# Pooling q inside the score product of the first batch, adding the pooled part while the output is turned back, and retuning modelled transfer times

## The chip, the cores and the metric

The kernel runs on one core of one Trainium2 chip. The metric is the device time of one execution in microseconds. Most versions were executed four times next to the kernel before on the same chip; medians are given.

## The reference, cut to what matters

```python
# q, k, v: [8 batches, 8 heads, 576 tokens, 64]
q_d = q.reshape(B, H, 144, 4, D).mean(axis=3)      # and k_d, v_d: pooled over 4 tokens
out_up    = repeat(softmax_attention(q_d, k_d, v_d), 4, axis=tokens)
out_local = attention over the tokens within distance 3
x = (out_up + out_local) as [8*576 tokens, 512]
h = x @ w_in                                        # 512 -> 2048
out = (h - tanh(h)) @ w_out                         # 2048 -> 512
```

## The kernel before

The kernel treats two heads at a time as a head pair: four pairs make one batch, p0 to p3 being batch 0. In SBUF, q and k of a pair lie interleaved in bf16 (`qk[..., token, 0 or 1]`), two heads stacked in the 128 partitions, so each head is a 64-row operand of TensorE. The dense part consumes x in blocks of 512 tokens, so its first block needs all four pairs of batch 0.

Pooling and pooled scores. VectorE or GpSimd pools q and k together in two adds (`add1`, `add2`), and then four products make the pooled scores:

```python
def s2(step=16):
    biased(480, 576, t2)
    for hh in range(2):
        score(4, hh, 0, t2)
    for i in range(2):
        for hh in range(2):
            rows = slice(64 * hh, 64 * hh + 64)
            c = 96 + G * i                          # G = 144
            T.matmul(two(t2)[:, hh, c:c + G], qkd[s][rows, step * i:step * i + 128, 1],
                     qkd[s][rows, 0:G, 0], start=True, stop=True)
```

Turning back in batch 0: six transposes on TensorE, a copy of the pooled part (`od`), and two joins on VectorE that add each pooled column to four tokens:

```python
for q0, n, t in [...]:
    T.transpose(flat()[:, q0:q0 + n], ln[s][0:n, t, :], ident[0:n, 0:n])
... od[s] <- flat()[:, 480:480 + G]                 # ACT or DVE
... xT[j] <- flat()[...] + od[s] broadcast by 4     # DVE, twice
```

From batch 1 on, the turning of q and k (`qr` to `qT`) and of the output (`ln` to `lT`) is done by transposing DMAs.

The order of the instructions is not written by hand. The kernel first collects all operations with a modelled duration each, simulates the engines and the DMA queue with these, and emits the instructions in the order that the simulation gives. Where an operation may run on more than one engine (`P.choice`), the simulation picks the engine too:

```python
P.dma("SP", 1340, lambda: nc.sync.dma_start_transpose(out=qT[s], in_=...), 1684, 92, ...)
#            modelled use of the DMA engines in ns, and of one piece of it ^^^^  ^^
T_QK, T_V, ... = (760, 864), (850, 939), ...        # loads: batch 0, later batches
```

On the chip each engine has its instructions in that fixed order, whether or not the data are there; the traces below show ScalarE stand 3.25 us before a copy whose data are late, with other work queued behind it.

The softmax here doesn't subtract the row's maximum and nothing guards it: scores larger than these inputs give would overflow.

## Time and profile before

| | before |
|---|---|
| time, median of the first three runs (range) | 321.28 us (321.06 to 322.15) |
| span of the profiled execution | 321.8 us (this execution took 323.51 us) |
| TensorE busy | 307.7 us, 96% |
| first dense matmul | 25.37 us |
| TensorE idle from there to 69.2 us | 2.42 us |
| TensorE idle from 69.2 to 270 us | 2.92 us |

The idle times are window lengths minus TensorE's busy time in the window. Some matmul records are missing from each trace: of the dense products 39 are missing before, counted against their weight loads, and such a hole can show as about 0.16 us of idle time with no cause. So the sums themselves are too high.

### The profile page before, as it was taken

The page shows a single profiled execution, that of the slowest core. Times are in us where ns is not written, and L with a number is a line of the kernel's source. Part 1 is how long each engine was busy: PE and PEld are TensorE (multiplying, and loading weights), DVE is VectorE, ACT ScalarE, POOL GpSimd, SP SyncE. Part 2 cuts the span into 40 slices and gives each one's busy share as a digit, 9 for nine tenths or more (in the row PEclk, how much of TensorE's full clock was granted, in tenths as well). Part 3 has the DMA queues.
Part 4 walks back from the last instruction along what each step waited for, and adds up shares of the span by engine and source line. Part 5 has one row for each costly group of instructions (what it writes and reads, how often), then busy time and mean ns, then how long its engine had stood idle before and what let it go on. Part 6 is the DMA issues. An engine that isn't in the chain of part 4 may idle for free.

```text
span 321.8 us, 6551 instructions
## 1 busy us (share of the span) xinstructions
PE 307.7 (96%) x2370; PEld 156.6 (49%) x2411; DVE 189.4 (59%) x345; ACT 202.1 (63%) x344; POOL 178.0 (55%) x223
## 2 busy tenths in 40 slices
PE   6889989999999999999999999999999999999995
PEld 2565534655455444544544444444444544444444
DVE  5777872658855873696458634964288428443300
ACT  3876955578876885687677456775488336444411
POOL 7384335562696878688876698859679110000000
PEclk9999999999999999999999999999999999999999
DMA  7999999994979999999999999999992220000021
GB/s 229 265 249 206 223 244 266 277 253 140 209 180 208 246 233 263 253 230 227 238 236 238 226 238 232 263 203 251 217 231 56 69 80 0 33 35 33 33 98 67
DMA packets 110814, 60.13 MB, mean 187 GB/s; under 512 B 87998, under 2 KB 98110, under 8 KB 110782
## 3 DMA queue, kind: packets, MB, share of 16 engines
q1 hardware_dynamic: 106270, 54.93, 72.4%
q0 software_dynamic: 4224, 4.19, 7.7%
q10 hardware_dynamic: 288, 0.59, 0.6%
q8 instruction: 19, 0.31, 0.4%
q14 instruction: 13, 0.11, 0.1%
HBM read 43.64 MB, written 9.44 MB: 165 GB/s over the span
## 4 chain that ended last, share of the span: by engine, by line
PE 62%; DMA 17%; POOL 6%; ACT 4%; issue 4%; SPq 3%; DVE 2%; POOLq 0%; ACTq 0%; DVEq 0%
PE bank L773 29%; PE bank L739 25%; DMA vst<-in_v_dram 7%; DMA qkn<-in_k_dram 6%; PE bank L651 3%; DMA qT<-qr 3%; POOL half L567 2%; PE bank L588 2%; SPq L428 1%; POOL qkd L572 1%; ACT qk L537 1%; POOL half L475 1%; DMA lT<-ln 1%; SPq L403 1%; ACT u L748 1%
## 5 line engine op out<-in xcount | busy, mean ns | idle before, releaser
L773 PE MATMUL bank<-w_out_sb,gT 128*128 128x512 bf16 (+1 forms) x572 | 133.3, 373 | 3.2 <-DVE gT L751 1.3
L739 PE MATMUL bank<-xT,w_in_sb 128*128 128x512 bf16 x557 | 132.6, 379 | 1.1 <-issue 0.3
L751 DVE TENSOR_TENSOR gT<-bank,u 128x512 bf16<-128x512 f32 x144 | 96.2, 687 | 49.4 <-ACT u L748 48.7
L748 ACT ACTIVATE u<-bank 128x512 f32<-128x512 f32 x144 | 84.5, 606 | 41.7 <-PE bank L739 37.9
L773 PEld LDWEIGHTS <-gT 128*128 128x128 bf16 x592 | 55.3, 98 | 61.2 <-issue 1.9
L739 PEld LDWEIGHTS <-w_in_sb 128*128 128x128 bf16 x576 | 54.3, 98 | 62.7 <-issue 0.2
L628 DVE TENSOR_TENSOR bank<-bank,bias 128x960 f32<-128x960 f32 (+1 forms) x56 | 41.3, 758 | 18.8 <-PE bank L588 17.8
L567 POOL TENSOR_TENSOR half<-qk 128x576 f32<-128x576 bf16 x28 | 32.1, 1145 | 32.4 <-ACT qk L537 13.4
L785 ACT COPY y<-bank 128x512 f32<-128x512 f32 (+1 forms) x37 | 21.3, 576 | 33.6 <-PE bank L773 28.4
L518 POOL CAST qr<-qkn 128x1152 bf16<-128x1152 f32 x28 | 32.0, 1145 | 12.0 <-DMA qkn<-in_k_dram 8.7
L632 ACT ACTIVATE E<-bank 128x960 bf16<-128x960 f32 x32 | 30.9, 971 | 12.2 <-DVE bank L628 12.2
L537 ACT COPY qk<-qT 128x1152 bf16<-128x1152 bf16 x22 | 26.8, 1217 | 9.9 <-DMA qT<-qr 9.5
L678 DVE TENSOR_TENSOR ln<-bank,r 128x768 bf16<-128x768 f32 x32 | 30.5, 957 | 1.0
L701 POOL TENSOR_TENSOR xT<-lT 128x480 bf16<-128x480 bf16 x22 | 22.3, 1012 | 15.2 <-DMA lT<-ln 15.2
L676 DVE RECIPROCAL r<-bank 128x12 f32<-128x12 f32 x32 | 7.2, 227 | 36.7 <-PE bank L651 32.7
L475 POOL TENSOR_TENSOR half<-v 128x512 f32<-128x512 f32 x20 | 26.0, 1299 | 1.3
L651 PEld LDWEIGHTS <-E 128*128 128x128 bf16 x576 | 21.7, 98 | 6.8 <-ACT E L644 0.2
L453 POOL CAST vw<-vst 128x640 bf16<-128x640 f32 x21 | 15.1, 724 | 14.4 <-DMA vst<-in_v_dram 14.4
L644 ACT ACTIVATE E<-bank 128x576 bf16<-128x576 f32 x32 | 21.4, 670 | 0.0
L572 POOL TENSOR_TENSOR qkd<-half 128x288 bf16<-128x288 f32 x30 | 19.9, 665 | 2.3 <-DVE half L567 0.8
L651 PE MATMUL bank<-vw,E 128*128 128x65 bf16 x320 | 21.0, 194 | 0.0
L588 PEld LDWEIGHTS <-qk 64*128 64x128 bf16 x320 | 9.2, 94 | 14.5 <-issue 9.8
(70 smaller groups left out, 187.6 us busy)
## 6 DMA issues: line engine op xcount, KB each, us to landing
vst<-in_v_dram SPq DMA_DIRECT2D x62, 160.0 KB, 4.2
qkn<-in_q_dram SPq DMA_DIRECT2D x32, 288.0 KB, 4.4
out_dram<-y SPq DMA_DIRECT2D x35, 256.0 KB, 2.6
qkn<-in_k_dram SPq DMA_DIRECT2D x30, 288.0 KB, 4.2
v<-in_v_dram SPq DMA_DIRECT2D x20, 256.0 KB, 3.5
w_in_sb<-in_moe_w_in_dram POOLq DMA_DIRECT2D x4, 512.0 KB, 13.1
w_out_sb<-in_moe_w_out_dram POOLq DMA_DIRECT2D x4, 512.0 KB, 17.7
v<-in_v_dram SPq DMA_DIRECT2D x20, 32.0 KB, 3.3
```

Source lines behind the costliest of these rows:

```text
L475: GP.tensor_tensor(out=v2, in0=v4[s][:, :, :, 0:128], in1=v4[s][:, :, :, 128:256], op=ALU.add)
L518: op("POOL", 1160, lambda: GP.tensor_copy(out=qr[s].rearrange("p a (h d) -> p h a d", h=2), in_=qkn[sn].rearrange("p h (a d) -> p h a d", ...
L537: op("ACT", 1095, lambda: A.copy(out=full.rearrange("p (g a) i -> p g a i", a=A9), in_=qT[s].rearrange("p a (g i) -> p g a i", i=2)), read ...
L567: eng.tensor_tensor(out=half, in0=four[:, :, 0:2, :], in1=four[:, :, 2:4, :], op=ALU.add)
L628: V.tensor_tensor(out=part, in0=part, in1=bias[:, lo:hi].unsqueeze(1) .to_broadcast([128, 2, hi - lo]), op=ALU.add)
L632: op("ACT", 860, lambda: A.activation(out=e1, in_=two(t1)[:, :, 0:480], func=AF.Exp, scale=SCALE), drain=[t1], writes=[("E", e, 0)], pri=pri)
L651: T.matmul(two(to)[0:m, hh, 65 * n:65 * n + 65], E[e][0:rhs.shape[0], c:c + m], rhs, start=first, stop=last)
L678: op("DVE", 880, lambda: V.tensor_tensor(out=ln[s].rearrange("p n (h d) -> p h n d", d=D), in0=blocks()[:, :, :, 0:64], in1=r[s].unsqueeze ...
L739: T.matmul(one(tok), w_in_sb[:, dc, fc * 128:(fc + 1) * 128], xT[dc][:, kb * 512:kb * 512 + 512], start=(dc == 0), stop=(dc == N_DC - 1))
L748: op("ACT", 490, lambda: A.activation(out=u[us], in_=one(tok), func=AF.Tanh), drain=[tok], writes=[("u", us)], pri=DPRI)
L751: op("DVE", 610, lambda: V.tensor_tensor(out=gT[g][:, fc, :], in0=one(tok), in1=u[us], op=ALU.subtract), drain=[tok], reads=[("u", us)], w ...
L773: T.matmul(one(tok)[:, 0:n], gT[g][:, fc, ts * 128:ts * 128 + 128], w_out_sb[:, fc, cols:cols + n], start=(fc == 0), stop=(fc == N_FF - 1))
```

## The change

The intent is to take work off VectorE and GpSimd in the stretch before the first dense matmul. For batch 0 TensorE pools q itself: four products with every fourth token of q accumulate in PSUM, so only k is pooled by adds. And the pooled part of the output is spread over four tokens by a product with a 0/1 matrix `up`, accumulated on top of the turned-back local part, so that one copy remains. Along with this come retuned modelled transfer times, a finer cut of the second dense block, and one load of v split in two.

```diff
 def s2(step=16):
-    for i in range(2):
-        for hh in range(2):
-            T.matmul(two(t2)[:, hh, c:c + G], qkd[s][rows, step * i:step * i + 128, 1],
-                     qkd[s][rows, 0:G, 0], start=True, stop=True)
+    for i in range(2):
+        for a in range(4 if only_k else 1):
+            for hh in range(2):
+                T.matmul(two(t2)[:, hh, c:c + G], qkd[s][rows, step * i:step * i + 128, 1],
+                         four[rows, :, a, 0] if only_k else qkd[s][rows, 0:G, 0],
+                         start=(a == 0), stop=(a == 3 or not only_k))
 ...   # add1, add2 only on k (take = slice(1, 2)) for p < 4; modelled cost of s2 370 + 480
+def back_up():                                     # p < 4
+    T.matmul(summed()[:, 0:512], ln[s][:, 4, :], up[:, 0:512], start=True, stop=False)
+    for t in range(4):
+        T.matmul(summed()[:, QW * t:QW * t + QW], ln[s][0:QW, t, :], ident[...], start=False, stop=False)
+    T.matmul(summed()[:, 480:512], ln[s][0:112, 5, :], up[0:112, 512:544], start=False, stop=True)
+    T.matmul(summed()[:, 512:576], ln[s][0:112, 5, :], up[0:112, 544:608], start=True, stop=True)
+P.choice([("ACT", 520, ... A.copy(out=xs, in_=summed()[:, 0:S])),
+          ("DVE", 620, ... V.tensor_copy(out=xs, in_=summed()[:, 0:S]))], ...)
 ...   # GpSimd builds up (c_up): 2 memsets, 7 selects
-T_QK, T_V, ... = (760, 864), (850, 939), ...
+T_QK, T_V, ... = (760, 832), (850, 904), ...
 ...   # turning DMAs: 1684 -> 1622, 1128 -> 1086 (pieces 92 -> 89); v4 loads: 1000 -> 936, 125 -> 119
 ...   # piece of a weight load: 240 -> 340
-cuts = (0, 2, 3, 4) if kb == 0 else (0, 2, 4)
+cuts = (0, 2, 3, 4) if kb < 2 else (0, 2, 4)
 ...   # first load of v: rows 0:124 -> rows 0:112 and 112:124
```

`four` is a view of the interleaved `qk`: one element of the moving operand every 4 tokens x 2 (q and k) x 2 bytes = 16 bytes. The old operand, pooled q in `qkd`, has one element every 4 bytes.

More of the change, by code (lines that the diff above doesn't have):

```diff
@@ L328 @@
     warm = lT[0].rearrange("p n c -> p (n c)")[:, 0:512]
+    up = lT[1].rearrange("p n c -> p (n c)")[:, 0:608]
     r = fixed("r", [128, 2, 6], FP32, 2)
@@ L361, in c_group, with c_up @@
                          base=3, pattern=[[4, 32]], channel_multiplier=-1)
+    def c_up():
+        GP.memset(up[:, 0:512], 1.0)
+        GP.affine_select(out=up[:, 0:512], in_=up[:, 0:512], compare_op=ALU.is_ge, fill=0.0,
+                         base=0, pattern=[[1, 512]], channel_multiplier=-4)
+        GP.affine_select(out=up[:, 0:512], in_=up[:, 0:512], compare_op=ALU.is_ge, fill=0.0,
+                         base=3, pattern=[[-1, 512]], channel_multiplier=4)
+        last = up[:, 512:608]
+        GP.memset(last, 0.0)
+        for base, mult in [(16, -1)] + [(-32 - a, -4) for a in range(4)]:
+            GP.affine_select(out=last, in_=last, compare_op=ALU.not_equal, fill=1.0,
+                             base=base, pattern=[[1, 96]], channel_multiplier=mult)
     def c_pick():
@@ L421, in issue @@
                 if b == 0 and h == 0:
-                    nc.sync.dma_start(out=t[4:128, i, 0, :], in_=v[b, h, 0:124, :])
+                    nc.sync.dma_start(out=t[4:116, i, 0, :], in_=v[b, h, 0:112, :])
+                    nc.sync.dma_start(out=t[116:128, i, 0, :], in_=v[b, h, 112:124, :])
                     nc.sync.dma_start(out=t[:, i, 1:5, :], in_=win(QW - 4, 128, 4))
@@ L447, in load_w @@
         keys = [(name, f, c) for c in range(4)]
-        P.dma("POOL", 780, issue, T_W + 1200 * (f == 0 and src is moe_w_in), 240, dst=keys, after=[after], pri=W_PRI)
+        P.dma("POOL", 780, issue, T_W + 1200 * (f == 0 and src is moe_w_in), 340, dst=keys, after=[after], pri=W_PRI)
     def prep_v(p):
@@ L467, in issue @@
                             ap=[[4 * D, n], [S * D, 2], [1, 4 * D]]))
-        load(480, lambda: issue(0, 128, 0), [("v4", s, 0)], 1000, 220, -30, 16)
-        load(420, lambda: issue(128, 16, 1), [("v4", s, 1)], 125, 125, -30, 2)
+        load(480, lambda: issue(0, 128, 0), [("v4", s, 0)], 936, 220, -30, 16)
+        load(420, lambda: issue(128, 16, 1), [("v4", s, 1)], 119, 119, -30, 2)
     def pool_v4(p):
@@ L534, in attention @@
             P.dma("SP", 1340, lambda: nc.sync.dma_start_transpose(
-                out=qT[s], in_=qr[s].rearrange("p a c -> p (a c)")), 1684, 92,
+                out=qT[s], in_=qr[s].rearrange("p a c -> p (a c)")), 1622, 89,
                   src=[("qr", s, 0), ("qr", s, 1)], dst=[("qT", s)], pri=-50, lead=500)
@@ L564, in attention @@
         adders = ADDERS[p >= NEARLY]
+        only_k = p < NP
+        take = slice(1, 2) if only_k else slice(0, 2)
         def add1(eng):
-            eng.tensor_tensor(out=half, in0=four[:, :, 0:2, :],
-                              in1=four[:, :, 2:4, :], op=ALU.add)
+            eng.tensor_tensor(out=half[:, :, :, take], in0=four[:, :, 0:2, take],
+                              in1=four[:, :, 2:4, take], op=ALU.add)
         def add2(eng):
             with nc.allow_low_precision("pooled q and k"):
-                eng.tensor_tensor(out=qkd[s][:, 0:G],
-                                  in0=half[:, :, 0, :],
-                                  in1=half[:, :, 1, :], op=ALU.add)
+                eng.tensor_tensor(out=qkd[s][:, 0:G, take],
+                                  in0=half[:, :, 0, take],
+                                  in1=half[:, :, 1, take], op=ALU.add)
         P.port.update((len(P.ops), len(P.ops) + 1))
-        P.choice([(name, n1, lambda eng=eng: add1(eng)) for name, n1, _, eng in adders],
+        P.choice([(name, n1 // (1 + only_k), lambda eng=eng: add1(eng))
+                  for name, n1, _, eng in adders],
                  reads=[("qk", s, 0), ("qk", s, 5)], writes=["half"], pri=pri)
-        P.choice([(name, n2, lambda eng=eng: add2(eng)) for name, _, n2, eng in adders],
+        P.choice([(name, n2 // (1 + only_k) + 40 * only_k, lambda eng=eng: add2(eng))
+                  for name, _, n2, eng in adders],
                  reads=["half"], writes=[("qkd", s)], pri=pri)
@@ L606, in s2 @@
             for i in range(2):
-                for hh in range(2):
-                    rows = slice(64 * hh, 64 * hh + 64)
-                    c = 96 + G * i
-                    T.matmul(two(t2)[:, hh, c:c + G], qkd[s][rows, step * i:step * i + 128, 1],
-                             qkd[s][rows, 0:G, 0], start=True, stop=True)
+                for a in range(4 if only_k else 1):
+                    for hh in range(2):
+                        rows = slice(64 * hh, 64 * hh + 64)
+                        c = 96 + G * i
+                        T.matmul(two(t2)[:, hh, c:c + G],
+                                 qkd[s][rows, step * i:step * i + 128, 1],
+                                 four[rows, :, a, 0] if only_k else qkd[s][rows, 0:G, 0],
+                                 start=(a == 0), stop=(a == 3 or not only_k))
         def s12():
@@ L636, in attention @@
         if p < MERGE:
-            op("PE", 370 + 110 * (p < NP), s2, slack=late, reads=qks + [("qkd", s)],
+            op("PE", 370 + 480 * (p < NP), s2, slack=late, reads=qks + [("qkd", s)],
                fill=[t2], pri=pri)
@@ L682, in attention @@
             op=ALU.mult), drain=[to], reads=[("r", s)], writes=[("ln", s)], pri=pri)
-        tb = P.psum(1, kind)
+        tb = P.psum(1, kind) if p >= NP else None
         def flat():
@@ L694, in attention @@
             P.dma("SP", 1260, lambda: nc.sync.dma_start_transpose(
-                out=lT[s], in_=ln[s].rearrange("p n c -> p (n c)")), 1128, 92,
+                out=lT[s], in_=ln[s].rearrange("p n c -> p (n c)")), 1086, 89,
                   src=[("ln", s)], dst=[("lT", s)], pri=-50, lead=500)
@@ L713, in attention, with summed @@
                      reads=[("lT", s)], writes=[("x", b, j)], pri=pri)
+            return
+        if p < NP:
+            tb = P.psum(2, kind)
+            def summed():
+                return two(tb).rearrange("p n c -> p (n c)")
+            def back_up():
+                T.matmul(summed()[:, 0:512], ln[s][:, 4, :], up[:, 0:512],
+                         start=True, stop=False)
+                for t in range(4):
+                    T.matmul(summed()[:, QW * t:QW * t + QW], ln[s][0:QW, t, :],
+                             ident[0:QW, 0:QW], start=False, stop=False)
+                T.matmul(summed()[:, 480:512], ln[s][0:112, 5, :], up[0:112, 512:544],
+                         start=False, stop=True)
+                T.matmul(summed()[:, 512:576], ln[s][0:112, 5, :], up[0:112, 544:608],
+                         start=True, stop=True)
+            op("PE", 500, back_up, slack=late, reads=[("ln", s), ("lT", 1), "ident"],
+               fill=[tb], pri=pri)
+            xs = xT[j][:, b * S:(b + 1) * S]
+            P.choice([("ACT", 520, lambda: A.copy(out=xs, in_=summed()[:, 0:S])),
+                      ("DVE", 620, lambda: V.tensor_copy(out=xs, in_=summed()[:, 0:S]))],
+                     drain=[tb], writes=[("x", b, j)], pri=pri)
             return
@@ L745, in mm1 @@
                reads=[("w_in", fc // 4, c) for c in range(4)] +
-               [("x", b, j) for b in bs for j in range(d1 if kb == 0 else NP)],
+               [("x", b, j) for b in bs for j in range(d1 if kb < 2 else NP)],
                writes=["dense"] * (kb == 0 and fc == 3 and d1 == 4), fill=[tok], pri=5000)
@@ L816 @@
     DPRI = -1
-    T_QK, T_V, T_W, W_PRI, NEARLY = (760, 864), (850, 939), 2750, 32, NP
+    T_QK, T_V, T_W, W_PRI, NEARLY = (760, 832), (850, 904), 2750, 32, NP
     CAST_V = [[("POOL", 770, GP.tensor_copy), ("ACT", 620, A.copy)],
@@ L829 @@
     op("POOL", 2700, c_bias, writes=["bias"], pri=-97)
+    op("POOL", 2500, c_up, writes=[("lT", 1)], pri=-50)
     for i in range(2):
```

## The prediction

> **What bounds the kernel now.** I read the page first, for the engine that fills the span.
>
> ```profile
> PE 307.7 (96%) x2370; PEld 156.6 (49%) x2411; DVE 189.4 (59%) x345; ACT 202.1 (63%) x344; POOL 178.0 (55%) x223
> ...
> PE   6889989999999999999999999999999999999995
> ...
> PEclk9999999999999999999999999999999999999999
> DMA  7999999994979999999999999999992220000021
> ```
>
> TensorE is 96% busy at full clock. The only slices below 9 are the first three, the sixth and the last (slices are 8.05 us): the attention of batch 0 must be done before any dense matmul can run, and the change touches exactly that stretch. The DMA engines are also full until about slice 30. Next I cut the span at the first dense matmul, at a gap near 49 us, and in pieces after that.
>
> ```profile
> core 0: us, PE busy (x) PEld busy (x) DVE busy (x) ACT busy (x) POOL busy (x), PEclk, DMA share, GB/s
> 0.00:25.37 25.37, 20.25 (x248) 12.06 (x251) 18.37 (x71) 16.29 (x29) 16.82 (x38) 1.00 1.01 246
> 25.37:49.00 23.63, 21.82 (x179) 11.04 (x180) 18.81 (x34) 18.10 (x35) 8.88 (x10) 1.00 1.20 226
> 49.00:69.20 20.20, 19.59 (x197) 11.69 (x201) 8.18 (x16) 11.41 (x20) 11.15 (x13) 1.00 0.98 281
> 69.20:120.00 50.80, 50.02 (x407) 25.46 (x413) 38.49 (x63) 40.28 (x69) 34.75 (x41) 1.00 0.94 201
> ```
>
> From 25.37 us on TensorE idles 1.81 us up to 49 us, then 0.61, 0.78, and 2.5 us in all from 120 to 318.5 us: 5.7 us together. So the end is the start of dense work plus a fixed queue of TensorE work (1152 full-size dense matmuls, which stream at about 0.216 us each in the chain of waits, are 249 us of it, the rest later attention) plus that idle time. The change can pay in two places only: an earlier first dense matmul, or less idle time after it. What decides the first one? The timeline at that point:
>
> ```profile
> 22.99 1.82 DVE L678 TENSOR_TENSOR ln<-bank,r 128x768 bf16<-128x768 f32 x2
> 24.97 0.49 PE L692 MATMUL bank<-ident,ln 120*128 120x120 bf16 x6
> 25.37 3.41 PE L739 MATMUL bank<-xT,w_in_sb 128*128 128x512 bf16 x15
> 26.65 0.81 DVE L722 TENSOR_TENSOR xT<-bank,od 128x480 bf16<-128x480 bf16 x2
> ```
>
> L692 turns the last head pair (p3) back, L739 is the dense input product. It starts when L692 has been issued; only its fourth operand, p3's (last row, done at 27.46), comes later, and meanwhile TensorE runs other operands. But L739 also needs weights, w_in in four parts, cast on the way by a GpSimd-issued DMA. First the two GpSimd rows that lead to it, then the landing time of the issue that starts at 15.67 (view of that tensor, cut to this issue).
>
> ```profile
> 15.01 0.72 POOL L453 CAST vw<-vst 128x640 bf16<-128x640 f32 x1 [2.16 <-DMA vst<-in_v_dram]
> 15.67 1.65 POOL L440 DMA_DIRECT2D w_in_sb<-in_moe_w_in_dram  x2
> ```
>
> ```profile
> DMA to landing us min/median/max: 9.7/9.7/9.7
> ```
>
> 15.67 + 9.7 = 25.37: the weights land in the very instant at which dense work starts. The other three landings, read the same way, are 12.2, 14.0 and 17.8 us after issues at about 16.6, 18.0 and 18.8, thus near 28.8, 32.0 and 36.6. So two things now end together at 25.4 us: the attention chain and the first weights. The issue waits on purpose for the load of v of pair 2 (2.16 us of waiting in its predecessor), which the change does not touch.
>
> The largest idle piece later:
>
> ```profile
> 45.06 0.73 ACT L453 CAST vw<-vst 128x640 bf16<-128x640 f32 x1 [2.13 <-DMA vst<-in_v_dram]
> ...
> 47.06 1.02 PE L773 MATMUL bank<-w_out_sb,gT 128*128 128x512 bf16 x4 [0.96 <-DVE gT L751]
> ```
>
> ScalarE stands in order before a cast whose v has not come; three tanh of block 0 queue behind it, so gT is late and the output product L773 waits (0.96, then another 0.33 us).
>
> **What the Trainium skill says.** "TensorE: Matmul & The Clock Gate", Part 3 (The mechanism): matmuls in different row groups run concurrently, starting about 4 ns apart. The trace agrees:
>
> ```profile
> 20.17 0.29 PE L610 MATMUL bank<-qkd 64*128 64x144 bf16 x4
> ```
>
> One of these takes 223 ns, so the fourth starts 0.29 - 0.22 = 0.07 us after the first: two pairs, 60 ns apart, 60 ns being 144 columns at the rate of L739 (512 in 0.216). The next instruction follows at 20.40, 0.23 us after the first. "SBUF — State Buffer", Door 1, says SBUF has 16-byte lines and an access that crosses to a new line pays; two hits per line are needed for full rate. The new q operand takes every fourth token of interleaved bf16 q and k, a step of 16 bytes: one hit per line. The old ones step by 4 bytes; no row here shows 16. The same page, Who interferes with whom: some two-input VectorE operations and GpSimd exclude each other. The trace agrees: the second pooling add took 0.94 us on VectorE from 9.08, beside a GpSimd cast, and 0.46 from 13.78, beside none.
>
> **The change part by part, pairs p0 to p3.**
> - Pooling of q leaves VectorE. Before: add 1 128x576 is 0.76, add 2 0.46 us, about 1.2 per pair. Half the elements: 0.4 + 0.25. Over four pairs some 2.3 us of VectorE/GpSimd time.
> - Scores: 4 products become 16. Twelve more are six pairs at 60 ns, +0.36 us per pair, 1.4 us in all, if the 16-byte step is free. If it halves the rate, eight pairs at 120 against two at 60 ns, +0.84, 3.4 us in all. Both lie before the first dense matmul, where TensorE idles or runs filler (17 filler products in the order before, 13 after).
> - Turning back: 6 transposes (0.33 us to issue) become 7 products of 512 + 480 + 32 + 64 columns, 1088 at 0.42 ns, 0.46 us. Then od (0.28) and two joins (0.82 + 0.25 before overlap) become one copy of 576 f32 columns. A ScalarE copy of 512 is 0.58, a VectorE operation on 512 f32 0.69; I estimate 0.7 us. Thus about 0.4 us less on the chain of each pair, and no two-step wait.
> - GpSimd builds the up-matrix after the bias: one memset and two selects on 512 columns (0.5 + 0.6 + 0.6, from the bias rows) and a memset and five selects of 96 (5 x 0.27): 3.3 us, from 5 to 8.4 us. The early casts of p0 and p1 that it did there go to ScalarE and VectorE instead, by the changed order. The clash with VectorE may cost p0 and p1 0.3 us.
> - Loads: the same bytes, one more small v issue. Later order changes because the modelled DMA times change.
>
> Now the chain with the changed instruction order. p3's k lands at about 13.5 as before. ScalarE no longer casts it (0.58), so exp of p2 starts near 13.9 instead of 14.16. TensorE has p1's 16 products at 12.4 to 12.9, p2's until 15.3; p3's transposes then run 15.3 to 15.8 (before 15.16 to 15.7). Two output products follow; scores of p3 at 17.5, its exp at 17.9 (before 18.19). Back-turn of p0, v pooling and 16 products bring TensorE to 19.8; p3's second exp ends at 20.8 (before 21.4), its output product at about 21.5 (before 22.3), both normalizations at 23.4 (before 24.8), back-turn at 24.0, a score step of pair 4 to 24.3. So all x could be ready by 24.7 and dense work could start near 24.3, 1.0 us earlier.
>
> But the weights. Their issue stays at 15.7, their landing at 25.4. I therefore give the earlier chain almost nothing: first dense matmul at 25.2 to 25.6.
>
> What remains is idle time. In the changed order all 16 tanh of block 0 stand before the cast that waits for v, and the joins of p2 and p3 (1.6 us of VectorE from 24.8) are gone when gT begins. That should remove most of the 1.3 us of waiting of L773. Blocks later should be neutral: same work, DMA full as before.
>
> Sum: 0 for the start, -1.1 for the stall, 0 for the rest: 321.28 - 1.1 = 320.2 us.
>
> **Rivals.**
> 1. The weights do not hold (w_in lands sooner, or the coincidence at 25.37 is chance): the full 1.0 us comes on top, 319.2. For it: L692 ended issuing only 0.08 us before. Against it: landing and start agree to 0.01 us.
> 2. The 16-byte step halves the products' rate: +0.48 us for each pair on a TensorE that p1 to p3 already queue on. The chain then ends at 25.5 to 26 instead of 24.3, and takes over from the weights: 320.4 to 320.9. Only the page speaks for it.
> 3. Supply: everything before 240 us is also near the DMA limit (share about 1). Dense work that runs ahead then waits for batch 1's x, or for w_in part 4 (lands 36.6; the new order wants it about 37.7, and GpSimd issues parts 2 to 4 about 1 us later). The gain is given back: 321.3, or 322 if a reordered queue is unlucky.
>
> **Range and chances.** Everything movable is about 2 us downwards (start and stall) and 1 us up, plus reordering noise of some 0.7 us in the 3.9 us of idle time after 49 us. Range 318.6 to 321.9. 2% is 6.4 us, more than all the idle time after the start: faster 0.02, same 0.96, slower 0.02.
>
> **What would show it.** The first L739 at 25.2 to 25.6 while the last copy of x is done before 25.2; w_in's first landing at that start. The 16 products: issue in 0.5 to 0.6 us if the step is free, about 1 us if not. No wait of L773 near 45 us, and TensorE idle from the first dense matmul to 49 us down from 1.81 to about 0.7. I am wrong if the first dense matmul comes before 24.8 or after 26, or if idle time after 69 us moves by over 1 us.

## More of the kernel before

The comparisons named e to h ran on four different chips, so a difference between medians of two comparisons is rough.

The windows of the kernel before from 120 us on (start and end, length, then busy time with instruction count of TensorE, its weight loads, VectorE, ScalarE and GpSimd, granted clock, DMA share, GB/s):

```profile
120.00:170.00 50.00, 49.42 (x401) 24.93 (x407) 30.09 (x47) 34.81 (x57) 41.10 (x49) 1.00 1.00 243
170.00:220.00 50.00, 48.89 (x366) 24.01 (x372) 31.71 (x51) 33.17 (x55) 38.64 (x45) 1.00 1.13 231
220.00:270.00 50.00, 49.55 (x346) 24.12 (x351) 27.41 (x43) 28.83 (x51) 26.65 (x33) 1.00 0.54 131
```

TensorE has almost no gap here. And one group of the page, ScalarE copying q and k from where the transposing DMA put them (busy time and mean ns, then idle time of the engine just before the group and what ended it):

```profile
L537 ACT COPY qk<-qT 128x1152 bf16<-128x1152 bf16 x22 | 26.8, 1217 | 9.9 <-DMA qT<-qr 9.5
```

Of the 22 copies some find their transposed data not yet landed; ScalarE stands 9.5 us in all. In this kernel that wait costs TensorE next to nothing.

## The result, and the profile after

The changed kernel takes **333.41 us** (median of 4 runs, 331.66 to 334.42) against 321.17 us (320.28 to 322.15) of the kernel before in the same comparison: ratio 1.0375, 95% interval 1.0321 to 1.0428, so slower by over 2%. Ratios are computed as the mean time of one kernel's fast runs over that of the other's of the same rounds, so not quite the ratio of the medians quoted beside them.

The page of the kernel after:

```profile
PE 316.4 (95%) x2418; PEld 159.8 (48%) x2459; DVE 188.1 (57%) x342; ACT 201.2 (60%) x339; POOL 181.5 (55%) x232
...
PE   6999999999999989999999798999999999999995
```

TensorE is still the full engine, but it does 8.7 us more, and the dips moved: the first slices are fuller, and there are new dips in the middle (slices 15, 23 and 25, of 8.3 us each). Its windows, cut at the new first dense matmul:

```profile
0.00:31.55 31.55, 28.03 (x298) 15.07 (x299) 17.97 (x71) 15.99 (x26) 18.42 (x44) 0.95 1.06 250
31.55:69.20 37.65, 37.33 (x332) 20.49 (x336) 24.13 (x42) 25.73 (x49) 18.52 (x21) 1.00 1.02 228
69.20:120.00 50.80, 49.20 (x412) 25.62 (x414) 35.62 (x59) 39.30 (x68) 34.01 (x41) 1.00 0.86 194
120.00:170.00 50.00, 48.51 (x405) 24.20 (x411) 29.89 (x48) 33.50 (x55) 40.17 (x46) 1.00 1.14 241
170.00:220.00 50.00, 46.47 (x342) 22.56 (x348) 32.08 (x52) 33.94 (x57) 38.96 (x46) 1.00 1.04 223
220.00:270.00 50.00, 47.84 (x365) 23.60 (x370) 27.35 (x44) 29.00 (x49) 31.45 (x39) 1.00 0.72 158
```

With these and the windows of before, the difference of the profiled spans (332.7 - 321.8 = 10.9 us) splits into the parts below. Idle time is what is left of a window, so the sum has to close; what the table tells is the split. The profiled execution of the changed kernel is the slowest of its four (334.42 us).

| | before | after | difference |
|---|---|---|---|
| first dense matmul | 25.37 | 31.55 | +6.18 |
| idle from there to 69.2 us | 2.42 | 0.32 | -2.10 |
| idle from 69.2 to 270 us | 2.92 | 8.78 | +5.86 |
| idle from 270 us to the end | 3.64 | 3.65 | 0.0 |
| TensorE busy after the first dense matmul | 287.44 | 288.40 | +0.96 |

So there are two losses of about the same size, a late start and late idle time, and one gain, the stall near 45 us that the prediction expected to vanish.

**The late start.** Rows of the timeline of the kernel after (start, length, engine, line, operation; in brackets the idle time before it and what ended that). Line 630 is the pooled products, 666 the exp of the pooled scores, 584 the first pooling add of p3 (128x288 is k alone), 757 the one copy of x that is left, 784 the dense input product:

```profile
10.38 2.21 PE L630 MATMUL bank<-qk,qkd 64*128 64x144 bf16 x16
12.62 0.65 ACT L666 ACTIVATE E<-bank 128x576 bf16<-128x576 f32 x1 [1.39 <-PE bank L630]
...
22.02 0.66 POOL L584 TENSOR_TENSOR half<-qk 128x288 f32<-128x288 bf16 x1 [5.54 <-ACT qk L569]
...
24.65 2.21 PE L630 MATMUL bank<-qk,qkd 64*128 64x144 bf16 x16
26.90 0.65 ACT L666 ACTIVATE E<-bank 128x576 bf16<-128x576 f32 x1 [1.70 <-PE bank L630]
...
30.50 1.59 DVE L757 CAST xT<-bank 128x576 bf16<-128x576 f32 x2
31.55 2.55 PE L784 MATMUL bank<-xT,w_in_sb 128*128 128x512 bf16 x11
```

The sixteen products of a pair take 2.21 us where I had expected 0.5 to 0.6, or 1 us at worst, and they do so in all four pairs. ScalarE waits for each of them (6.4 us in all), the whole chain of batch 0 is pushed back, and the last copy of x ends at 32.09 instead of 27.46 us. The first weights are no longer what holds: issued at 15.56 and landing 8.4 us later, they are there at 23.96. One thing besides the products differs: TensorE's granted clock in this profile was 0.50 from about 15.4 to 18.7 us, with TensorE busy all the while, and 1.00 in the profile of before. Up to about 1.7 us of the late start may be the clock (an estimate: half of these 3.3 us).

**The late idle time.** The same two views as before, first the groups of the page:

```profile
L784 PE MATMUL bank<-xT,w_in_sb 128*128 128x512 bf16 x558 | 135.3, 379 | 5.2 <-DVE gT L796 4.3
...
L552 ACT COPY qk<-qT 128x1152 bf16<-128x1152 bf16 x22 | 26.7, 1214 | 19.6 <-DMA qT<-qr 16.3
```

ScalarE now stands 16.3 us before the copies of transposed q and k, against 9.5, and TensorE stands 4.3 us before dense input products, waiting for VectorE's gT to free a PSUM bank; in the kernel before there was no such wait after 69 us. That the two belong together is seen in the longest one (timeline of the kernel after; line 793 is tanh, 796 is gT = h - tanh h):

```profile
182.65 1.17 ACT L552 COPY qk<-qT 128x1152 bf16<-128x1152 bf16 x1 [3.25 <-DMA qT<-qr]
183.73 1.57 ACT L793 ACTIVATE u<-bank 128x512 f32<-128x512 f32 x3
184.35 1.89 DVE L796 TENSOR_TENSOR gT<-bank,u 128x512 bf16<-128x512 f32 x3 [2.89 <-ACT u L793]
185.10 0.81 PE L784 MATMUL bank<-xT,w_in_sb 128*128 128x512 bf16 x3 [1.84 <-DVE gT L796]
```

Read it downwards: the transposing DMA is late, the copy that needs it stands first in ScalarE's queue, three tanh queue behind it and then run without a wait of their own, VectorE has no tanh to subtract, no bank comes free, and TensorE stands 1.84 us. The other three waits for gT (0.86, 0.30 and 1.31 us, ending at 117.32, 218.69 and 250.18 us) come the same way: each ends some 2.5 us after the start of such a copy (at 114.84, 216.24 and 247.72 us) that had waited 2.24, 1.10 and 2.27 us for its DMA. The landing time of these transposing DMAs was 4.5 us in the median before (3.5 to 5.4) and 5.1 us after (3.2 to 6.9); the modelled time for them had been lowered.

### The profile page after: what moved, and what is told of

Its sections match the earlier page's. It is cut to its first block, busy times and chain, and to the rows that moved or that the text cites. A ratio compares the mean times of both kernels' runs of the same rounds, so it can differ in the third digit from the quotient of the medians.

```text
span 332.7 us, 6660 instructions
## 1 busy us (share of the span) xinstructions
PE 316.4 (95%) x2418; PEld 159.8 (48%) x2459; DVE 188.1 (57%) x342; ACT 201.2 (60%) x339; POOL 181.5 (55%) x232
## 5 line engine op out<-in xcount | busy, mean ns | idle before, releaser
L784 PE MATMUL bank<-xT,w_in_sb 128*128 128x512 bf16 x558 | 135.3, 379 | 5.2 <-DVE gT L796 4.3
L818 PEld LDWEIGHTS <-gT 128*128 128x128 bf16 x592 | 56.0, 98 | 61.6 <-issue 0.3
L584 POOL TENSOR_TENSOR half<-qk 128x576 f32<-128x576 bf16 (+1 forms) x29 | 32.8, 1130 | 48.7 <-ACT qk L569 28.4
L552 ACT COPY qk<-qT 128x1152 bf16<-128x1152 bf16 x22 | 26.7, 1214 | 19.6 <-DMA qT<-qr 16.3
L468 POOL CAST vw<-vst 128x640 bf16<-128x640 f32 x22 | 16.3, 744 | 12.6 <-DMA vst<-in_v_dram 12.5
L589 POOL TENSOR_TENSOR qkd<-half 128x288 bf16<-128x288 f32 (+1 forms) x29 | 19.1, 660 | 1.1
```

The source lines that it names most:

```text
L552: op("ACT", 1095, lambda: A.copy(out=full.rearrange("p (g a) i -> p g a i", a=A9), in_=qT[s].rearrange("p a (g i) -> p g a i", i=2)), read ...
L584: eng.tensor_tensor(out=half[:, :, :, take], in0=four[:, :, 0:2, take], in1=four[:, :, 2:4, take], op=ALU.add)
L784: T.matmul(one(tok), w_in_sb[:, dc, fc * 128:(fc + 1) * 128], xT[dc][:, kb * 512:kb * 512 + 512], start=(dc == 0), stop=(dc == N_DC - 1))
L818: T.matmul(one(tok)[:, 0:n], gT[g][:, fc, ts * 128:ts * 128 + 128], w_out_sb[:, fc, cols:cols + n], start=(fc == 0), stop=(fc == N_FF - 1))
```

## The experiments

All kernels agree with the reference within the tolerance of the comparison, also those that compute a wrong pooled q. Theories at the start: **step** (the 16-byte step of the moving operand makes the products slow), **count** (sixteen products instead of four are the cost, whatever their step), **turning back** (the new product and copy cost), **order** (the new modelled times make a worse order). First the whole in one table, sorted by what was changed. "Products" is the length of the row of pooled products of one pair, "qT wait" is how long ScalarE stood for the transposing DMA between 69 and 270 us.

| kernel | q pooled by | modelled times | time, us | ratio to before | products, us | first dense, us | qT wait, us |
|---|---|---|---|---|---|---|---|
| before | adds | old | 321.17 to 323.61 | 1 | 0.29 (4) | 25.37 | 9.5 |
| after | TensorE, 16 B | lowered | 333.41 | 1.0375 | 2.21 (16) | 31.55 | 16.3 |
| e1_q_step4 | TensorE, 4 B (wrong) | lowered | 328.47 | 1.0219 | 0.68 (16) | 24.36 | 20.3 |
| e2_turn_only | adds | lowered | 328.31 | 1.0204 | | 24.95 | 17.6 |
| e3_q_only | TensorE, 16 B | old | 329.70 | 1.0242 | 2.21 (16) | 30.01 | 8.1 |
| e4_tuning_only | adds | lowered | 327.62 | 1.0205 | | 24.73 | 17.1 |
| f2_times_only | adds | lowered | 327.17 | 1.0174 | | 24.15 | 18.8 |
| f3_cuts_only | adds | old | 321.87 | 1.0005 | | 27.90 | 2.7 |
| f4_turn_old_times | adds | old | 321.20 | 0.9996 | | 25.62 | 6.1 |
| g1_after_old_times | TensorE, 16 B | old | 327.12 | 1.0169 | 2.21 (16) | 31.33 | 6.2 |
| g2_times_up | adds | raised | 324.20 | 1.0057 | | 27.46 | 2.5 |
| g3_turn_early_w | adds | old | 322.74 | 1.0039 | | 24.74 | 1.4 |
| h1_times_loads | adds | loads lowered | 327.26 | 1.0166 | | 24.53 | 9.8 |
| h2_times_turns | adds | turning lowered | 325.70 | 1.0109 | | 25.70 | 9.8 |
| h3_times_wpiece | adds | weight piece only | 321.91 | 1.0003 | | 24.27 | 5.4 |

The medians of the kernel before in the five comparisons were 321.17, 321.73 (e), 322.18 (f), 321.97 (g) and 323.61 us (h); those of f and h include one slow run each (324.89 and 325.81 us), which the ratios leave out. f1 and g4 are measurements of single products, with one run each, whose state is unknown.

Two things are read from the table. The five kernels with all modelled times lowered are the ones that wait longest for the transposing DMA (16.3 to 20.3 us, against 1.4 to 9.8 us in the others). And a late start need not cost its whole length: in the profile of f3 the clock was 0.50 from about 8.0 to 14.9 us and the first dense matmul came at 27.90, yet its span, 321.2 us, is no longer than the 321.8 us of the kernel before.

### e1_q_step4: the change with only the step of q made 4 bytes

```diff
-four[rows, :, a, 0]                   # every 4th token: 16 bytes
+full[rows, G * a:G * a + G, 0]        # 144 tokens in a row: 4 bytes, the wrong tokens
```

The order of all instructions on all engines is the same as in the changed kernel, and so are their number and sizes; the result is wrong.

> The changed kernel, every instruction in the same order on every engine; only the q operand of the 16 pooled products is now 144 neighbouring tokens (a step of 4 bytes) in place of every fourth token (16 bytes). The result is wrong on purpose. Theory (the 16-byte step makes the moving read slow): the 16 products of a pair take 0.5 to 0.6 us instead of 2.1 us, one of them about 223 ns instead of 432, the first dense matmul comes back from 31.6 to about 25.4 us, and the time falls to 319 to 322 us if the later idle time is a consequence of the late start, or to about 326 us if the later idle time (about 4.7 us) belongs to the new order. Rival (four products accumulating into one PSUM region, or 16 in a row with their weight loads, are slow in themselves): still 2.1 us, 432 ns, and 333 us.

Measured: 328.47 us (327.71 to 329.84), ratio 1.0219 (1.0186 to 1.0253), 4.9 us less than the changed kernel. Rows of its timeline:

```profile
9.99 0.68 PE L630 MATMUL bank<-qk,qkd 64*128 64x144 bf16 x16
...
24.36 2.55 PE L784 MATMUL bank<-xT,w_in_sb 128*128 128x512 bf16 x11
```

Sixteen products at 4 bytes take 0.68 us, at 16 bytes 2.21; the first dense matmul comes 7.2 us earlier. Up to the next instruction a row takes 0.62 us here and 2.14 in the changed kernel, so the four rows make 6.1 of the 7.2 us; the rest may be the clock, which was 1.00 in this profile up to that point. (The profiles are the fastest of this kernel's runs and the slowest of the changed kernel's, so their difference is larger than that of the medians.) So it is the step and not the count that makes the late start, since nothing else differs in the programs. The count alone costs 0.62 - 0.23 = 0.39 us per pair, close to the +0.36 that the prediction had for a free step. What remains is slower than before by about 2% (the interval reaches below 2%) although it starts 1.0 us earlier than before: its late idle time is there in full (TensorE stands 4.3 us for gT in this kernel too). The two losses are separate.

### e2_turn_only, e3_q_only, e4_tuning_only: each part by itself

e2 is the change without the pooling of q; e3 is the kernel before plus only the pooling of q; e4 is the kernel before with only the new modelled times, the cuts and the split load.

```diff
 e2 (on after):   -only_k = p < NP
                  +only_k = False                 # and modelled cost of s2 370 + 110
 e3 (on before):  +only_k = p < NP ... take ... the loop over a in s2, cost 370 + 480
 e4 (on before):  T_QK, T_V, turning, v4 and weight times, kb < 2, v split as in the change
```

> The changed kernel with q pooled on VectorE again (four products per pair, as before); the turning back with the pooled part added by TensorE, and the modelled transfer times, stay. Theory (the loss is the strided products): first dense matmul at 25 to 26 us, time 319 to 322.5 us. Rival (the turning back with 7 products and one 576-column copy, or the building of its matrix on GpSimd, costs by itself): above 324 us, with the late x copies visible before the first dense matmul.

> The kernel before with the pooling of q moved to the score product and nothing else (its turning back, modelled transfer times and dense cuts unchanged). Theory: four times 1.9 us more on TensorE before the first dense matmul, which comes 5 to 7 us later than 25.4; time 327 to 334 us. If the strided products hurt only together with the new turning back or the new order, it stays within 323 us.

> The kernel before with only the modelled transfer times, the split of one v load and the finer cuts of the second dense block: no changed arithmetic. Theory (these only reorder, and the late idle time comes from the late start): 320 to 323 us. Rival (the new order starves TensorE from 90 to 260 us by itself): 325 to 327 us, with TensorE idle time after 69 us at some 8 us as in the changed kernel instead of 3 us.

Measured: 328.31, 329.70 and 327.62 us, ratios 1.0204 (1.0141 to 1.0268), 1.0242 (1.0179 to 1.0305) and 1.0205 (1.0164 to 1.0247). e3 has the slow products (2.21 us in each pair) and a first dense matmul at 30.01, and no late stall to speak of (0.8 us of TensorE waits with a named cause after 69 us). e4 has none of the new work, starts 0.6 us earlier than before, and still loses 2%, with ScalarE standing 17.1 us for the transposing DMAs. So the first theory written down for e4 (320 to 323 us) fell: the tuning that came along with the change costs about as much as the slow products, and e2, above 324 us but without the late copies of x expected for that, cannot tell whether the turning back costs anything, since the tuning is in it. That had to be taken apart.

### f1_ladder and g4_ladder_alone: one product at different steps

f1 replaces the two groups of eight products of each pair by reads of one step each, and gives wrong scores. In g4 the steps 4, 8, 12 and 16 bytes stand side by side in p0 and p1 with the two heads (row groups of TensorE) taken in turn, and in p2 and p3 again with four products of one row group followed by four of the other.

```diff
-four[rows, :, a, 0]
+read(p, i, hh)     # full[rows, 0:144*k:k, 0] for a step of 4*k bytes, k = 1..4; 8 and 16 by a permuted view
```

> The changed kernel with the q operand of the pooled products read at other steps, eight products each, all 144 columns on 64 rows: pair 0 at 4 then 8 bytes, pair 1 at 12 then 16, pair 2 at 32 then 64 (in 2 and 4 runs), pair 3 at 2 bytes (another tensor), then at 16 bytes with the four products of one row group in a row and then those of the other, so that no two run side by side. Wrong result on purpose. The skill page's rule (two hits per 16-byte line for full rate): 2, 4 and 8 bytes at 0.24 us per eight (60 ns per pair), 12 bytes in between, 16 bytes and more at 1.07 us per eight (266 ns per pair). If instead the cost grows with the step in bytes, 8 bytes is already dearer than 4, and 32 and 64 dearer than 16. Alone in the array: 16-byte products at 266 ns each, 2.1 us for the eight, if the rate belongs to the single stream; about 133 ns each, 1.07 us, if two streams at once are what halves it.

> The changed kernel with the pooled products read at 4, 8 (pair 0), 12, 16 bytes (pair 1), eight products each with the two row groups side by side, and the same four steps (pairs 2 and 3) with the four products of one row group in a row, then those of the other. Wrong result on purpose. From the first ladder: side by side 0.25, 0.51, 0.76, 1.03 us per eight. If TensorE's moving read takes about 0.89 ns for each 16-byte line, shared by the two row groups, the products alone take the larger of that and the streaming rate of 60 ns: 0.49 us per eight at 4 and 8 bytes, 0.76 at 12, 1.03 at 16. If each row group has its own read rate, 8 bytes alone is as dear per product as side by side per pair: 128 ns, 1.02 us per eight.

Rows of f1's timeline (eight products each), with steps of 4, 8, 12, 16 and 32 bytes from top to bottom:

```profile
10.29 0.42 PE L648 MATMUL bank<-qk,qkd 64*128 64x144 bf16 x8
10.56 0.68 PE L652 MATMUL bank<-qk,qkd 64*128 64x144 bf16 x8
12.80 0.93 PE L648 MATMUL bank<-qk,qkd 64*128 64x144 bf16 x8
13.55 1.20 PE L652 MATMUL bank<-qk,qkd 64*128 64x144 bf16 x8
16.45 1.20 PE L648 MATMUL bank<-qk,qkd 64*128 64x144 bf16 x8
```

About 0.165 us of each row is the fixed time of the last product (the product at 4 bytes takes 223 ns, of which about 60 are streaming, as the prediction worked out). What is left over eight products is 32, 64, 96, 129 and 129 ns on average for a product of 144 columns; the products start in pairs, so two run side by side and a pair takes twice these times. A step of 64 bytes gave 1.16 us, a step of 2 bytes 0.41. So of the steps measured 4 bytes is the largest that costs nothing; from there the cost grows in proportion to the step up to 16 bytes and then stays. That fits a cost for each 16-byte line touched, about 2 x 129 / 144 = 1.8 ns per line for a pair of products; it is inferred from these lengths. Neither of the two rules written down for f1 came whole: 8 bytes is dearer than 4, and 32 and 64 bytes are no dearer than 16. The row of g4 for 8 bytes, grouped by row group, and its row for 16 bytes:

```profile
17.61 0.70 PE L651 MATMUL bank<-qk,qkd 64*128 64x144 bf16 x8
...
23.03 1.21 PE L651 MATMUL bank<-qk,qkd 64*128 64x144 bf16 x8
```

They are 0.68 and 1.20 us with the row groups in turn: the grouped order takes the same time (f1's grouped row at 16 bytes, 1.19 us, too). The test says no more than that. In the trace the grouped products also start in pairs (two within 23.02 to 23.05 us, the next two not before 23.27), so no row shows one stream alone, and whether the streams of the two heads share reads of SBUF is left open. Of the values written down for g4's grouped rows, those of a shared read came roughly at 8, 12 and 16 bytes (0.49, 0.76 and 1.03 us; the rows less 0.165 are 0.54, 0.78 and 1.05) and not at 4 bytes (0.49; 0.28 was measured). In g4 the clock was 0.50 until about 11.7 us, but its rows begin at 12.07 and all ran at 1.00. Only the third pair's row in the changed kernel begins at a lowered clock (at 18.46, with 0.50 until about 18.7 us); it took 2.23 us against 2.21 in the others. That is one pair of products at 16 bytes that half the clock did not slow by more than 0.02 us; for the other steps nothing is shown.

### f2_times_only, f3_cuts_only, f4_turn_old_times: the tuning and the turning back apart

```diff
 f2 (on before): only the modelled times: (760, 832), (850, 904), 1622/89, 1086/89, 936, 119, piece 340
 f3 (on before): only cuts = (0, 2, 3, 4) if kb < 2 else (0, 2, 4)
 f4 (on before): only the new turning back; q pooled by adds, old times, old cuts, old load of v
```

> The kernel before with only the modelled transfer times changed (no cuts, no split load): a pure reordering. If these times make the order that starves TensorE late, 326 to 329 us with 8 us of idle time after 69 us; if not, 320 to 323 us.

> The kernel before with only the finer cuts of the second dense block. If the cuts make the starving order, 326 to 329 us; if not, 320 to 323 us. If both this and the run with the modelled times are slow, any reordering of the tuned kernel loses some 2%, and neither part is guilty by itself.

> The new turning back alone on the kernel before, with its modelled times, cuts and v load, q pooled on VectorE. If the loss is strided products plus the modelled times, this one is free of both: 319 to 322 us. If any reordering loses, 326 to 329 us.

Measured: f2 327.17 us (ratio 1.0174, 1.0123 to 1.0224), f3 321.87 (1.0005), f4 321.20 (0.9996, 0.9945 to 1.0046). Modelled times alone, numbers that never run on the chip, cost some 5 us. The waits of ScalarE in f2 between 69 and 270 us (total, number, longest):

```profile
ACT qk L537 <- DMA qT<-qr: 18.8, 9, 3.9
```

Twice as much as in the kernel before, whose instructions are the same ones in another order (345 on VectorE, 344 on ScalarE and 223 on GpSimd in both). In f4 the x of batch 0 is ready early, and what the first dense matmul then waits for is named in its timeline:

```profile
25.62 0.82 PE L783 MATMUL bank<-xT,w_in_sb 128*128 128x512 bf16 x3 [1.29 <-DMA w_in_sb<-in_moe_w_in_dram]
```

The new turning back does shorten the chain, and the wait for the weights takes that away, as predicted; g3 below shows that weights which come earlier bring no time either.

### g1_after_old_times, g2_times_up, g3_turn_early_w: the check from the other side, and a way out

```diff
 g1 (on after):  old modelled times, old cuts, old load of v; both parts of the change stay
 g2 (on before): modelled times raised by 3.7% instead: (760, 896), (850, 974), 1746/95, 1170/95, 1064, 131
 g3 (on f4):     first part of w_in issued one load of v earlier (after v of p1 instead of p2)
```

> The changed kernel (both the pooled products at 16 bytes and the new turning back) with the modelled transfer times, the cuts and the v load of the kernel before. If the loss is the sum of two separate causes, strided products (+5 to 6 us until the first dense matmul, seen as 31.6 against 24.4 us when only the step was changed) and the modelled times (+5 to 6 us of late idle time), then this one has only the first: 326 to 328.5 us, first dense matmul at 30 to 32 us. If the late idle time comes with late starts in any order, 331 to 334 us.

> The kernel before with the modelled transfer times raised by the 3.7% by which the change lowered them (loads 896 and 974 in place of 864 and 939, turning transfers 1746 and 1170 in place of 1684 and 1128). If the lowered times lose because an order that counts on faster transfers than the chip's makes TensorE stand before attention steps whose data are late, raised times cost little: 320 to 324 us. If the tuned times are a narrow optimum and any other order loses, 325 to 329 us here too.

> The new turning back alone (q pooled on VectorE, old times), with the first part of w_in issued after the load of v of pair 1 in place of pair 2. In the run without this, TensorE waited 1.3 us for these weights before the first dense matmul. If that wait is the last one there, the first dense matmul comes about 1 us earlier (24.3 to 24.8 us) and the time falls by 0.5 to 1 us, to about 320.5; if the weights only take bandwidth from k and v of pairs 2 and 3, no gain or a loss of 1 us.

Measured: g1 327.12 us (1.0169, 1.0104 to 1.0234), g2 324.20 (1.0057, 1.0012 to 1.0103), g3 322.74 (1.0039, 0.996 to 1.0118). Taking the tuning out of the changed kernel gives back 6.3 us (medians of two comparisons), and ScalarE's wait falls to this:

```profile
ACT qk L551 <- DMA qT<-qr: 6.2, 5, 3.3
```

Together with e1 this nearly closes the sum: 6.3 us for the tuning and 4.9 us for the step are 11.2 of the 12.2 us lost. g1 also shows that the late start needs no lowered clock: its clock was 1.00 up to the first dense matmul, which came at 31.33 us, against 0.95 on average in the profile of the changed kernel. What the clock added there is not shown, since the order is another one. Raised times make ScalarE wait little (2.5 us), yet that order is not better but slightly worse, and 324.20 us lies just between the two ranges written down for it. Its first dense matmul came at 27.46 us, 2.1 us later; 1.3 us of that was there when p1's transposes began (9.40 instead of 8.09 us), and the rest stands beside a clock of 0.50 from about 10.4 to 13.8 us, so it can't be put down to the order alone. g3 brought the first dense matmul to 24.74 us (its clock was 0.50 from about 12.1 to 15.6 us) without any gain in time. I found no version that beats the kernel before.

### h1_times_loads, h2_times_turns, h3_times_wpiece: which of the modelled times

Each changes one group of f2's times alone on the kernel before: the loads of q, k and v; the transposing DMAs; the piece of a weight load.

```diff
 h1: T_QK 864 -> 832, T_V 939 -> 904, v4 1000 -> 936 and 125 -> 119
 h2: turning 1684/92 -> 1622/89 and 1128/92 -> 1086/89
 h3: piece of a weight load 240 -> 340
```

> The kernel before with only the modelled times of the loads (q, k, v parts) lowered to those of the changed kernel; the turning transfers and the pieces of the weights keep their old ones. Theory A (the loads alone make the starving order): 326 to 328 us, TensorE idle between 120 and 220 us of 4 us or more. Theory B (the turning transfers do): 320.5 to 323 us, that idle near the kernel before's 1.7 us.

> Only the modelled times of the turning transfers lowered. Theory A (the loads do it): 320.5 to 323 us. Theory B (the turning transfers do it): 326 to 328 us with 4 us or more of TensorE idle between 120 and 220 us. If this and the run of the loads alone both stay under 324 us, it takes the combination.

> Only the modelled time of a piece of the weights changed. Both theories: 320.5 to 323 us, since no weight piece was seen to hold up TensorE after 70 us. If it gives 326 to 328 us both fall, and the order of the weights' pieces among the attention's transfers is the cause.

Measured: 327.26 us (1.0166, 1.0072 to 1.0259), 325.70 (1.0109, 1.0028 to 1.019) and 321.91 (1.0003, 0.991 to 1.0096); the kernel before scattered more than elsewhere in this comparison (320.21 to 325.81). Only the third is clear: no effect of the weight piece is seen. The first hit the time written down for theory A but not its sign, since TensorE's idle time from 120 to 220 us was 1.6 us and not 4 or more, and the second lies between both theories. ScalarE's wait for the transposing DMA is 9.8 us in both, as in the kernel before. The traces of h1 to h3 lack no record of the dense input product (the kernel before: 19 of 576), so their idle times are not raised by holes and can't be set beside the kernel before's 1.7 us; the named waits of TensorE from 120 to 220 us are 1.4 us in h1 and 0.4 in the kernel before. Their stalls are other ones: in h1 one of 2.17 us at 47.9 us, where a transposition stands in TensorE's queue before its cast by GpSimd is done, and a clock of 0.89 in the 10 us after it; in h2 three waits for pooled q and k (1.7 us together) and two for gT (1.5 us). The engines are partly other ones too (227 instructions on GpSimd in h1, 225 in h2, 223 before). So each group of lowered times gives an order with stalls of its own, the costs do not add up (1.66% and 1.09% alone, 1.74% together), and the long waits for the transposing DMA come only when both groups are lowered. Why h1 is as slow as f2 is left open.

## Why the prediction was wrong, point by point

- **The shape of the sum** (start of dense work plus a fixed queue plus idle time) can't fail, since idle time is the rest. But its terms are not independent: f3 started 2.5 us later than the kernel before (27.90 against 25.37 us) and its span was no longer (321.2 against 321.8 us). What failed were two of its terms.
- **The sixteen products were the mis-sized term.** The working itself took the 16-byte step as free ("issue in 0.5 to 0.6 us", 0 us for the start). The dearer case stood beside it as "If it halves the rate, eight pairs at 120 against two at 60 ns, +0.84, 3.4 us in all", and as rival 2, worth 320.4 to 320.9 us. That rival had the right cause, and its size was off by more than two: eight pairs at about 2 x 128 = 256 ns, which is +1.9 us per pair (2.14 from the first product to the next instruction, against 0.23) and 7.6 us over four pairs; the first dense matmul came 6.2 us later. I took "SBUF — State Buffer", Door 1, as saying that two hits per line give full rate, and concluded that one hit gives half. The ladder shows that in these products two hits per line (8 bytes) already halve it and one hit quarters it.
- **"Later order changes because the modelled DMA times change" and then "Blocks later should be neutral: same work, DMA full as before"** was the second failed step. The work was the same and the DMA engines were as full, but the order was another one, and engines that take their queue in order stand idle where a transfer lands later than the model had it; modelled transfers 4% shorter were enough: +5.9 us between 69 and 270 us, 6.3 us in time (g1). That the order alone can cost this is shown by f2; that it costs through late transposing DMAs is seen where all times were lowered, but not in h1 and h2, which lose 1.7% and 1.1% without longer waits for them, so it is not the whole account. The prediction had allowed 0.7 us for all reordering, and nothing in the trace of before supported that figure. It had even named the sign to look for ("if idle time after 69 us moves by over 1 us").
- **The weights pin the start at about 25 us:** right. e2, e4 and f4 show a first dense matmul at 24.7 to 25.6 us with a wait for w_in before it. With the same wait f2 and h3 start at 24.15 and 24.27 and h2 at 25.70 us, so the range of 25.2 to 25.6 was too narrow. In the changed kernel the chain grew past them, as rival 2 said it would, only by 6 us and not by less than one.
- **The stall at 45 us goes:** right, and more than predicted. Idle time from the first dense matmul to 69.2 us fell from 2.42 to 0.32 us. The late start is not needed for it: in e1, which starts at 24.36 us, it is 0.37.
- **The turning back saves some time that is hidden:** right (f4 at 0.9996). The copy was estimated at 0.7 us and took 0.75.
- **Small terms:** the first pooling add took 0.46 us (0.4 estimated), the second 0.42 to 0.44 instead of 0.25, so halving its elements from 0.46 us saved almost nothing, and one beside GpSimd took 0.88. The up-matrix took GpSimd 3.8 us (3.3 estimated).
- **The range and the chances** asked only how much idle time the change could remove ("2% is 6.4 us, more than all the idle time after the start"). That bounds a gain. It does not bound a loss, and 0.02 for slower was not earned by any line of the profile.

## What to carry to other kernels

Before folding a reduction into TensorE's moving operand, look at the step of that operand in bytes and not only at the number of columns: here a 16-byte step cost four times a 4-byte one and ate more than the saved adds. When the order of instructions comes from a model, a retuned constant of the model is a change of its own: measure it alone, and look for an engine that stands in order before one late transfer with ready work queued behind it. A bound on what can be gained says nothing of what can be lost.

## What the Trainium skill lacked or had wrong

- "SBUF — State Buffer", Door 1 (16-byte lines, at least two hits per line for full bandwidth): for the moving operand of a 64-row bf16 product of 144 columns, two hits per line were not enough. Steps of 4, 8, 12 and 16 bytes took 32, 64, 96 and 129 ns per product, 32 bytes as much as 16; of these only 4 bytes, four hits per line, ran at full rate, and the rest fits a cost per 16-byte line, about 1.8 ns for a pair of products running together (inferred).
- "TensorE: Matmul & The Clock Gate", Part 3 (The mechanism), gives the concurrency of row groups without what a strided read of the moving operand does to it: products of two row groups at a 16-byte step took 2.21 us for sixteen against 0.68 at 4 bytes, and taking the row groups in turn or in blocks of four made no difference (0.68 and 0.70 us for eight at 8 bytes), with products starting in pairs in both.
- I found no page that says how far the landing of a transposing DMA between two places of SBUF scatters under load, which a planned order depends on: 3.5 to 5.4 us before and 3.2 to 6.9 us after, with medians of 4.5 and 5.1.
